# A 64-channel chunk kept as two token halves on 128 partitions, its first layer in array halves, and other due times

## The chip, the cores and the metric

The kernel runs on one core of a Trainium2 chip. The metric is the device time of one execution in microseconds (us), the median of three runs for the kernel before. "PE" is the tensor engine, "ACT" the scalar engine, "DVE" the vector engine, "POOL" the GpSimd engine, and "SP" the engine that only issues transfers here. A PE instruction is either a weight load (LDWEIGHTS) or a matmul (MATMUL).

## The reference

```python
def _A_ref(u, log_A_real, A_imag, C_real, C_imag, log_dt, D_skip):
    dt = jnp.exp(log_dt)
    A = -jnp.exp(log_A_real) + 1j * A_imag
    C = (C_real + 1j * C_imag) * dt[:, None]
    P = jnp.exp((A * dt[:, None])[:, :, None] * pos[None, None, :])
    K = 2.0 * jnp.einsum("dn,dnl->dl", C, P).real
    ...          # y = causal convolution of u with K over 2048 positions
    return y + u * D_skip[None, None, :]

def _B_ref(x, w1, b1, w2):
    h = jnp.einsum("bsd,df->bsf", x, w1) + b1
    sp = jnp.log1p(jnp.exp(-jnp.abs(h))) + jnp.where(h > 0, h, jnp.zeros_like(h))
    act = h * jnp.tanh(sp)
    return jnp.einsum("bsf,fd->bsd", act, w2)

x = A_u                                    # 1 x 2048 x 640
xn = _layernorm(x, axis=-1)
return x + _A_ref(xn, ...) + _B_ref(xn, B_w1, B_b1, B_w2)   # w1 640 x 1728, w2 1728 x 640
```

## The kernel before

The 2048 tokens are handled in four blocks (`b`) of 512; CA and CB are the first and the last 256 tokens of a block. The 640 input channels are five slices (`k`) of 128. The 1728 hidden channels are 14 chunks (`f`): 13 of 128 and, as `f` = 8, one of 64.

To keep float32 accuracy with float16 products, each operand is a high part plus a low part, and a product is three: high by high, low by high, high by low. So a full chunk of the first layer is 15 matmuls of 128x512 into one PSUM bank, and the same for the second layer, which adds into five banks ACC that hold the block's output. In blocks 1 to 3 the chunks 0 to 7 and 9 to 12 are taken two at a time (`PAIRS`); such a pair is computed from seven smaller products of sums of weights and sums of inputs, in parts called `one`, `two`, `three_a`, `three_b` and `four`, of 12, 15, 9, 9 and 9 matmuls of 128x256. Between them ACT copies two results out (`cV`, line 1063, and `cY`, line 1064) before `two` may start, and DVE adds them up (`z`, line 1067, before `three_a`; `w`, line 1071, before `four`). Chunks 8 and 13 of every block, and all of block 0, go one at a time.

Behind each first-layer chunk runs a chain on ACT and DVE: a sigmoid (`sig`), its product with the biased value (`mul`), three more activations (`mish_a1` to `a3`), a product (`mish_v3`), and the split into a high part (`mish_a4`) and a low part (`mish_v4`), which the second layer reads three chunks later.

The chunk of 64 channels has its high and low weights side by side in one 128-wide tile. Its five high-input products are full 128x512 matmuls: the result's partitions 0 to 63 hold the high-weight part, 64 to 127 the low-weight part. The five low-input products have only 64 weight columns, and are laid into the two column halves of the array, two at a time. So one sum stands on 64 partitions by 512 tokens, in two pieces: `half_a` (ACT) copies the upper piece down, `half_v` (DVE) adds the two, and all of the chain works on 64 partitions by 512 tokens. `mish_a4` writes the high part twice, into both partition halves of two tiles, since the second layer wants high and low side by side.

The order of all work after the first 20.8 us is made by a planner (`Plan`) when the program is built. The PE order is written out by hand in `whole`; for ACT, DVE, POOL and SP the planner takes, of what is ready, the operation with the earliest due time. Due times come backwards from the PE order and from numbers written in `whole`: the scan of the state-space part (`skip_a` to `skip_e`, 20 slices of 512 tokens) is spread between `edge` marks, the parameter sums (`mode_ops`) and the checks on the weights (`chk`) have marks of their own. A general path that runs when a check fails stands behind the rest, and isn't taken here.

The PSUM banks H[0], H[1] and TR hold first-layer results. PZ, the place of a pair's last sum, is the CB half of H[0]; chunk 8 uses all of H[1] in block 0 and all of H[0] later.

Of the kernel before, what the change touches and what calls it, by code (L numbers as in the profile page):

```python
# [16 lines left out]
AF = mybir.ActivationFunctionType  # L17
OP = mybir.AluOpType
AX = mybir.AxisListType

P = 128
# [4 lines left out]
TB = 512  # L26
NB = L // TB
NT = TB // P
KD = D // P
FC = [P] * 8 + [64] + [P] * 5  # L30
# [5 lines left out]
PAIRS = (0, 2, 4, 6, 9, 11)  # L36
# [6 lines left out]
MA, MG, MD, MC = -6.52763197, 0.11462477, 0.92081132, 5.9480018 / -6.52763197  # L43
# [16 lines left out]
class Plan:  # L60
# [392 lines left out]
def body(ctx: ExitStack, tc: tile.TileContext, x, xT, logA, Aim, Cr, Ci, logdt, vec, w1, w1T, w2, w2T, out):  # L453
# [58 lines left out]


    TR, *H = (ps.tile([P, TB], F32, name=n) for n in ("tr", "h0", "h1"))
    PV, PX, PZ, PY, PW = TR[:, CA], TR[:, CB], H[0][:, CB], H[1][:, CA], H[1][:, CB]
    PVS = tmp.tile([P, TB // 2], F32, name="pvs")
    ACC = [ps.tile([P, TB], F32, name=f"acc{k}") for k in range(KD)]
    XT, ACT, SM, NX = ({} for _ in range(4))
# [272 lines left out]
    def mm1(b, f):  # L791
        h = bank(b, f)
        n = FC[f]
        xh, xl = XH[b % 2], XL[b % 2]
        hh, lh, hl = ([(h, w[f][:, k], x[k]) for k in range(KD)] for w, x in ((W1H, xh), (W1L, xh), (W1H, xl)))
        if n < P:

            low = [(h[n * (k % 2):n * (k % 2 + 1)], w[:, :n], x) for k, (_, w, x) in enumerate(hl[:-1])]
            _, w, x = hl[-1]
            low += [(h[n * j:n * (j + 1), c], w[:, :n], x[:, c]) for j, c in enumerate((CA, CB))]  # L800
            order = hh[:1] + low + hh[1:]
        elif b == 0:
            order = hh + hl + lh
        else:
            order = [t for pair in zip(hh, lh) for t in pair] + hl
        for j, (o, w, x) in enumerate(order):
            pe.matmul(o, w, x, start=(j == 0), stop=(j == len(order) - 1))  # L807
# [73 lines left out]
        pe.matmul(o, W2H[f][:, c], lo, start=False, stop=f == LAST)  # L881


    def src(b, f):
        return pl["A", b, f][:FC[f]] if FC[f] < P else bank(b, f)

    def half_a(b, f):
        n = FC[f]
        a.copy(pl["A", b, f][:n], bank(b, f)[n:2 * n])

    def half_v(b, f):
        n = FC[f]
        v.tensor_tensor(pl["A", b, f][:n], bank(b, f)[:n], pl["A", b, f][:n], op=OP.add)

    def sig(b, f, h=None, c=slice(0, TB)):
        n = FC[f]
        a.activation(pl["s", b, f][:n, c], src(b, f) if h is None else h, AF.Sigmoid, bias=cv[:n, f:f + 1], scale=1 / SH)  # L897

    def mul(b, f, h=None, c=slice(0, TB)):
        n = FC[f]  # L900
        v.scalar_tensor_tensor(pl["A", b, f][:n, c], src(b, f) if h is None else h, bs[:n, f:f + 1], pl["s", b, f][:n, c],  # L901
                               op0=OP.add, op1=OP.mult)

    def mish_a1(b, f):
        n = FC[f]
        a.activation(pl["p", b, f][:n], pl["s", b, f][:n], AF.Arctan, bias=one[:n], scale=-1.0)  # L906

    def mish_a2(b, f):
        n = FC[f]
        p = pl["p", b, f][:n]  # L910
        a.activation(p, p, AF.Square, bias=pi4[:n], scale=2.0)  # L911

    def mish_a3(b, f):
        n = FC[f]
        p = pl["p", b, f][:n]
        a.activation(p, p, AF.Tanh, bias=mb[:n], scale=MG)  # L916

    def mish_v3(b, f):
        n = FC[f]
        A = pl["A", b, f][:n]  # L920
        v.scalar_tensor_tensor(A, pl["p", b, f][:n], MC, A, op0=OP.add, op1=OP.mult)  # L921

    def mish_a4(b, f):
        n = FC[f]
        A = pl["A", b, f][:n]
        hi = pl["h", b, f][0]
        ACT[f] = hi, None
        a.activation(hi[:n], A, AF.Copy, scale=MA * SA / SH)  # L928
        if n < P:
            hi2 = pl["h", b, f][1]  # L930
            ACT[f] = hi, hi2
            a.activation(hi2[n:2 * n], A, AF.Copy, scale=MA * SA / SH)

    def mish_v4(b, f):
        n = FC[f]
        A = pl["A", b, f][:n]
        hi, hi2 = ACT[f]
        lo = pl["h", b, f][1] if n == P else hi[n:2 * n]
        v.scalar_tensor_tensor(lo, A, MA * SA / SH, hi[:n], op0=OP.mult, op1=OP.subtract)  # L939
        ACT[f] = hi, lo if n == P else hi2  # L940

    def drain(b, k, src, t=slice(0, TB)):
        z = XT[b][:, k, t]
# [3 lines left out]
    def whole():  # L947

        A, V, M, S, G = "ACT", "DVE", "PE", "SP", "POOL"
        M5, M2 = 0.2157, 0.11  # L950
        add = lambda name, eng, cost, fn, *args, **kw: pl.add(name, eng, cost, lambda: fn(*args), **kw)
        nothing = lambda: None
        PAIRED = [f + j for f in PAIRS for j in range(2)]
# [2 lines left out]
        def chain(b, f, pre, drop=()):  # L956

            n = (b, f)
            if FC[f] < P:
                add(("hc", *n), A, 0.55, half_a, b, f, pre=pre, take=("A", ("A", *n), 1))  # L960
                add(("ha", *n), V, 0.62, half_v, b, f, pre=[("hc", *n)])
                add(("sg", *n), A, 0.64, sig, b, f, pre=[("ha", *n)], take=("s", ("s", *n), 2))
                add(("v1", *n), V, 0.68, mul, b, f, pre=[("sg", *n)], drop=[("s", *n)])
            elif b > 0 and f in PAIRS:
                add(("sX", *n), A, 0.36, sig, b, f, PX, CA, pre=[("two", *n)], take=("s", ("s", *n), 2))
                add(("vX", *n), V, 0.38, mul, b, f, PX, CA, pre=[("sX", *n)], take=("A", ("A", *n), 1))
                add(("sg", *n), A, 0.36, sig, b, f, PZ, CB, pre=[("three_b", *n), ("sX", *n)])
                add(("v1", *n), V, 0.38, mul, b, f, PZ, CB, pre=[("sg", *n), ("vX", *n)], drop=[("s", *n)])
            else:
                add(("sg", *n), A, 0.60, sig, b, f, pre=pre, take=("s", ("s", *n), 2))  # L970
                add(("v1", *n), V, 0.68, mul, b, f, pre=[("sg", *n)], take=("A", ("A", *n), 1), drop=[("s", *n)])
            add(("a1", *n), A, 0.63, mish_a1, b, f, pre=[("sg", *n)], take=("p", ("p", *n), 1), drop=[("s", *n)])
            add(("a2", *n), A, 0.63, mish_a2, b, f, pre=[("a1", *n)])
            add(("a3", *n), A, 0.63, mish_a3, b, f, pre=[("a2", *n)])
            add(("v3", *n), V, 0.61, mish_v3, b, f, pre=[("a3", *n), ("v1", *n)], drop=[("p", *n)])
            add(("a4", *n), A, 0.54 if FC[f] == P else 1.1, mish_a4, b, f, pre=[("v3", *n)], take=("h", ("h", *n), 1))
            add(("v4", *n), V, 0.62, mish_v4, b, f, pre=[("a4", *n)], drop=[("A", *n)])

        def second(b, f, parts):

# [35 lines left out]
            chain(0, f, [("m1", 0, f)])  # L1016
        for f in range(3, NF):
            prev = {3: 0, 4: 1}.get(f, f - 2)
            add(("m1", 0, f), M, 15 * M5 if FC[f] == P else 1.85, mm1, 0, f,
                pre=[("hw1", f), ("ow1", f), ("v1", 0, prev), ("sg", 0, prev)] if f > 3 else [("v1", 0, prev), ("sg", 0, prev)])  # L1020
            chain(0, f, [("m1", 0, f)])
            if f == 7:
                add(("spread", 1), M, 0.1, spread, pre=[("rs", 1)])
            for o in second(0, f - LAG, []):
                o()
# [5 lines left out]
        for b in range(1, NB):  # L1031
            for f in range(NF):
# [4 lines left out]
                h2 = (b, f + 1 - LAG) if f + 1 >= LAG else (b - 1, NF + f + 1 - LAG)  # L1037
                if f not in PAIRS:
                    pb = before(b, f)
                    add(("m1", *n), M, 15 * M5 if FC[f] == P else 1.85, mm1, b, f,  # L1040
                        pre=[("v1", b, f - 2), ("sg", b, f - 2)])
# [345 lines left out]
```

## Time and profile before

| what | us |
|---|---|
| three runs | 358.28, 358.29 (median), 358.55 |
| the profiled execution, its own time | 358.88 |
| its span, first to last instruction | 357.3 |
| PE busy in the span | 351.0 |
| DVE, ACT, POOL busy | 311.3, 296.4, 50.5 |
| mean granted clock of PE | 1.000 |

The profiled execution took 358.88 - 357.3 = 1.58 us outside its span, and was 0.59 us longer than the median. The views used are the page, the waits, the chain that ended last in order of time, the groups by shape, and stretches of the timeline. A row of the timeline is start, length, engine, line, operation, tiles and shape, then the count of instructions merged into it; lengths overlap, since an engine begins the next instruction before the last has fully ended, so the distance between two starts tells the pace.

### The profile page before, as it was taken

What the parts mean: (1) busy time and instruction counts of PE and PEld (TensorE: products, weight loads), DVE (VectorE), ACT (ScalarE), POOL (GpSimd) and SP (SyncE); (2) the same over time, 40 slices, a digit from 0 to 9 for tenths busy, and PEclk for the clock granted to TensorE, in tenths of its full rate; (3) what the DMA queues carried; (4) which work ended last, traced back from release to release, by engine and by line L of the source; (5) the groups of instructions that cost most, each with busy time, mean ns of one, the idle gap of its engine ahead of it and who ended that gap; (6) DMA issues with size and microseconds to landing.
All of it is one profiled execution on the core that took longest, in us unless ns stands there. A gap on an engine that the chain in (4) does not pass through costs nothing.

```text
span 357.3 us, 6015 instructions
## 1 busy us (share of the span) xinstructions
PE 351.0 (98%) x2167; PEld 211.6 (59%) x2167; DVE 311.3 (87%) x585; ACT 296.4 (83%) x614; POOL 50.5 (14%) x72
## 2 busy tenths in 40 slices
PE   7999999999999999999999999999999999999996
PEld 6754444444666665666566666466566666567543
DVE  4989989999998999999999997899997988775552
ACT  3599999978487799889989987989988989878750
POOL 2100020000004041100103343100002462000000
PEclk9999999999999999999999999999999999999999
DMA  7889975205109954902255973951110995302004
GB/s 222 293 240 281 348 225 163 113 1 172 50 3 199 318 177 120 292 35 57 60 183 112 187 208 93 246 204 35 33 35 4 160 194 125 81 0 33 0 4 151
DMA packets 26052, 48.75 MB, mean 136 GB/s; under 512 B 3592, under 2 KB 6944, under 8 KB 26016
## 3 DMA queue, kind: packets, MB, share of 16 engines
q1 hardware_dynamic: 19168, 34.21, 29.9%
q0 software_dynamic: 6240, 13.11, 17.9%
q10 hardware_dynamic: 608, 0.98, 0.9%
q8 instruction: 19, 0.31, 0.4%
q14 instruction: 17, 0.14, 0.2%
HBM read 39.10 MB, written 5.26 MB: 124 GB/s over the span
## 4 chain that ended last, share of the span: by engine, by line
PE 95%; DMA 2%; DVE 1%; ACT 1%; issue 0%; ACTq 0%
PE acc L859 48%; PE h L827 18%; PE h L807 14%; PE tr L827 12%; DMA w<-in_w_dram 2%; PE h L789 1%; PE tr L789 1%; PE acc L1251 0%; DVE st L627 0%; PE acc L873 0%; PE acc L870 0%; PE acc L871 0%; ACTq L1271 0%; DVE st L628 0%; ACT w1h L552 0%
## 5 line engine op out<-in xcount | busy, mean ns | idle before, releaser
L859 PE MATMUL acc<-hi,w2h 128*128 128x512 f16 x273 | 100.9, 379 | 0.0
L859 PE MATMUL acc<-hi,w2l 128*128 128x512 f16 (+1 forms) x265 | 99.7, 379 | 0.0
L859 PE MATMUL acc<-lo,w2h 128*128 128x512 f16 x253 | 93.3, 379 | 0.0
L859 PEld LDWEIGHTS <-w2h 128*128 128x128 f16 x526 | 51.2, 98 | 48.5 <-issue 1.3
L897 ACT ACTIVATE s<-h,cv 128x512 f32<-128x512 f32 (+1 forms) x51 | 30.9, 605 | 23.7 <-PE h L827 18.4
L827 PEld LDWEIGHTS <-w1h 128*128 128x128 f16 x432 | 42.3, 98 | 10.7
L921 DVE SCALAR_TENSOR_TENSOR A<-p,A 128x512 f32<-128x512 f32 (+1 forms) x56 | 38.4, 685 | 7.2 <-ACT p L916 7.0
L859 PEld LDWEIGHTS <-w2l 128*128 128x128 f16 x273 | 25.6, 98 | 30.8 <-issue 1.1
L906 ACT ACTIVATE p<-s,kc 128x512 f32<-128x512 f32 (+1 forms) x56 | 40.1, 716 | 0.5
L916 ACT ACTIVATE p<-p,kc 128x512 f32<-128x512 f32 (+1 forms) x56 | 40.1, 715 | 0.2
L911 ACT ACTIVATE p<-p,kc 128x512 f32<-128x512 f32 (+1 forms) x56 | 40.0, 714 | 0.2
L939 DVE SCALAR_TENSOR_TENSOR lo<-A,hi 128x512 f16<-128x512 f32 x52 | 35.5, 682 | 3.6 <-ACT hi L928 3.3
L901 DVE SCALAR_TENSOR_TENSOR A<-h,bs,s 128x512 f32<-128x512 f32 (+1 forms) x51 | 33.1, 649 | 6.2 <-ACT s L897 5.9
L928 ACT ACTIVATE hi<-A 128x512 f16<-128x512 f32 (+1 forms) x56 | 35.0, 624 | 3.6 <-DVE A L921 3.4
L548 POOL DMA_DIRECT2D r<-in_xT_dram x15 | 13.7, 1099 | 126.0 <-ACT r L770 60.3
L807 PEld LDWEIGHTS <-w1h 128*128 128x128 f16 (+1 forms) x174 | 15.3, 99 | 20.3 <-issue 3.3
L749 DVE TENSOR_TENSOR_SCAN g<-g,car,kc 128x512 f32<-128x512 f32 x20 | 25.6, 1280 | 1.1 <-ACT g L743 1.1
L827 PEld LDWEIGHTS <-w1l 128*128 128x128 f16 x216 | 21.1, 98 | 8.4 <-issue 0.3
L753 DVE TENSOR_TENSOR_SCAN g<-g,car,g 128x512 f32<-128x512 f32 x20 | 25.6, 1279 | 0.1
L827 PE MATMUL tr<-xh,w1h 128*128 128x256 f16 x90 | 24.5, 272 | 0.1
L827 PE MATMUL tr<-xh,w1l 128*128 128x256 f16 x90 | 24.5, 273 | 0.0
L827 PE MATMUL tr<-xl,w1h 128*128 128x256 f16 x90 | 24.5, 273 | 0.0
(174 smaller groups left out, 730.1 us busy)
## 6 DMA issues: line engine op xcount, KB each, us to landing
w<-in_w_dram SPq DMA_DIRECT2D x23, 320.0 KB, 4.4
w<-in_w2T_dram SPq DMA_DIRECT2D x15, 288.0 KB, 6.5
w<-in_B_w_dram SPq DMA_DIRECT2D x13, 320.0 KB, 4.0
w<-in_w1T_dram SPq DMA_DIRECT2D x13, 320.0 KB, 6.7
x<-in_A_u_dram SPq DMA_DIRECT2D x12, 320.0 KB, 4.9
xt<-in_xT_dram SPq DMA_DIRECT2D x15, 256.0 KB, 5.6
r<-in_xT_dram POOLq DMA_DIRECT2D x15, 256.0 KB, 6.2
xt<-r POOLq DMA_DIRECT2D x15, 256.0 KB, 3.9
```

What stands on the lines that cost most here:

```text
L749: v.tensor_tensor_scan(g1[:, 1:], g1[:, 1:], zero.to_broadcast([P, TB]), car[:, 1, k:k + 1], op0=OP.add, op1=OP.add)
L807: pe.matmul(o, w, x, start=(j == 0), stop=(j == len(order) - 1))
L827: pe.matmul(o, p, q, start=start and n == 1, stop=n == 3 * len(w), skip_group_check=True)
L859: pe.matmul(o, w, x, start=start, stop=stop)
L897: a.activation(pl["s", b, f][:n, c], src(b, f) if h is None else h, AF.Sigmoid, bias=cv[:n, f:f + 1], scale=1 / SH)
L901: v.scalar_tensor_tensor(pl["A", b, f][:n, c], src(b, f) if h is None else h, bs[:n, f:f + 1], pl["s", b, f][:n, c], op0=OP.add, op1=OP.mult)
L906: a.activation(pl["p", b, f][:n], pl["s", b, f][:n], AF.Arctan, bias=one[:n], scale=-1.0)
L911: a.activation(p, p, AF.Square, bias=pi4[:n], scale=2.0)
L916: a.activation(p, p, AF.Tanh, bias=mb[:n], scale=MG)
L921: v.scalar_tensor_tensor(A, pl["p", b, f][:n], MC, A, op0=OP.add, op1=OP.mult)
L928: a.activation(hi[:n], A, AF.Copy, scale=MA * SA / SH)
L939: v.scalar_tensor_tensor(lo, A, MA * SA / SH, hi[:n], op0=OP.mult, op1=OP.subtract)
```

## The change

The chunk of 64 channels is laid out otherwise. Its 15 products (high by high, low by high, high by low, for five slices) all have 64 weight columns now, and each is done twice: tokens CA into partitions 0 to 63 through one column half of the array, tokens CB into partitions 64 to 127 through the other, both into the CA columns of the bank. So there are 30 matmuls of 64x256 instead of 5 of 128x512, 4 of 64x512 and 2 of 64x256. The sum stands on 128 partitions by 256 columns at once: `half_a` and `half_v` go, the chain works on 128x256, and only `mish_a4` and `mish_v4` go back to 64 partitions, in four and two instructions of 64x256 instead of two and one of 64x512. PZ moves to the CA half of H[0]. In the planner the costs of this chunk's operations are new, `mode_ops` are due before the last chunk of block 0 instead of before chunk 4 of block 1, four of the five scan marks move, and the checks' window goes from chunk 4 of block 1 to chunk 11 of block 3 over to chunk 6 of block 1 to chunk 8 of block 3. Lines of the changed kernel stand up to 14 lower.

```diff
-    PV, PX, PZ, PY, PW = TR[:, CA], TR[:, CB], H[0][:, CB], H[1][:, CA], H[1][:, CB]
+    PV, PX, PZ, PY, PW = TR[:, CA], TR[:, CB], H[0][:, CA], H[1][:, CA], H[1][:, CB]
...
         if n < P:
-            low = [(h[n * (k % 2):n * (k % 2 + 1)], w[:, :n], x) for k, (_, w, x) in enumerate(hl[:-1])]
-            _, w, x = hl[-1]
-            low += [(h[n * j:n * (j + 1), c], w[:, :n], x[:, c]) for j, c in enumerate((CA, CB))]
-            order = hh[:1] + low + hh[1:]
-        elif b == 0:
+            for i, (_, w, x) in enumerate(hh + lh + hl):
+                for j, c in enumerate((CA, CB)):
+                    pe.matmul(h[n * j:n * (j + 1), CA], w[:, :n], x[:, c], start=i == 0, stop=i == 3 * KD - 1)
+            return
+        if b == 0:
...
-    def half_a(b, f):
-        n = FC[f]
-        a.copy(pl["A", b, f][:n], bank(b, f)[n:2 * n])
-
-    def half_v(b, f):
-        n = FC[f]
-        v.tensor_tensor(pl["A", b, f][:n], bank(b, f)[:n], pl["A", b, f][:n], op=OP.add)
...
+    def cols(f):
+        return slice(0, TB) if FC[f] == P else CA
...
     def mish_a4(b, f):
...
+        for t in (hi[:n], lo[n:2 * n]):
+            for j, c in enumerate((CA, CB)):
+                a.activation(t[:, c], A[n * j:n * (j + 1), CA], AF.Copy, scale=MA * SA / SH)
     def mish_v4(b, f):
...
+        for j, (c, h) in enumerate(((CA, hi[:n]), (CB, lo[n:2 * n]))):
+            v.scalar_tensor_tensor(hi[n:2 * n, c], A[n * j:n * (j + 1), CA], MA * SA / SH, h[:, c], op0=OP.mult, op1=OP.subtract)
...
+        HALF1 = 1.84
...
-            if FC[f] < P:
-                add(("hc", *n), A, 0.55, half_a, b, f, pre=pre, take=("A", ("A", *n), 1))
-                add(("ha", *n), V, 0.62, half_v, b, f, pre=[("hc", *n)])
...
-            add(("m1", 0, f), M, 15 * M5 if FC[f] == P else 1.85, mm1, 0, f,
+            add(("m1", 0, f), M, 15 * M5 if FC[f] == P else HALF1, mm1, 0, f,
...
-                due=start(1, 4))
+                due=start(0, 13))
...
-        edge = [start(1, 4), start(2, 0), start(2, 11), start(3, 5), start(3, 11)]
+        edge = [start(0, 13), start(2, 0), start(2, 8), start(3, 8), start(3, 13)]
...
-        t0, t1 = start(1, 4), start(3, 11)
+        t0, t1 = start(1, 6), start(3, 8)
```

What the planner makes of it is shown at three places. The first is PE at the beginning of chunk 8 in block 0 (`w1h8` are the chunk's weights, `xh00` to `xh04` and `xl00` to `xl04` the high and low inputs of the five slices, `h1` the bank). Before:

```order
L807 LDWEIGHTS w1h8_121
L807 MATMUL h1_212<-xh00_168,w1h8_121 128x512
L807 LDWEIGHTS w1h8_121
L807 MATMUL h1_212<-xl00_178,w1h8_121 64x512
L807 LDWEIGHTS w1h8_121
L807 MATMUL h1_212<-xl01_179,w1h8_121 64x512
L807 LDWEIGHTS w1h8_121
L807 MATMUL h1_212<-xl02_180,w1h8_121 64x512
```

and now:

```order
L800 LDWEIGHTS w1h8_121
L800 MATMUL h1_212<-xh00_168,w1h8_121 64x256
L800 LDWEIGHTS w1h8_121
L800 MATMUL h1_212<-xh00_168,w1h8_121 64x256
L800 LDWEIGHTS w1h8_121
L800 MATMUL h1_212<-xh01_169,w1h8_121 64x256
L800 LDWEIGHTS w1h8_121
L800 MATMUL h1_212<-xh01_169,w1h8_121 64x256
```

Each 64-column load now serves a matmul of 256 tokens, and nothing in the chunk is 128 columns wide any more.

The second is ACT in block 1 around the copies of the second pair (chunks 2 and 3): `pvs<-tr` is `cV`, `h1<-tr` is `cY`, `p1` is the chain of an earlier chunk. Before:

```order
L897 ACTIVATE s1_243<-h1_212,cv_102 128x512
L906 ACTIVATE p1_248<-s1_243,kc_89 128x512
L928 ACTIVATE hi2_253<-A2_246 128x512
L911 ACTIVATE p1_248<-p1_248,kc_89 128x512
L1063 COPY pvs_213<-tr_210 128x256
L1064 COPY h1_212<-tr_210 128x256
L916 ACTIVATE p1_248<-p1_248,kc_89 128x512
```

and now:

```order
L890 ACTIVATE s1_243<-h1_212,cv_102 128x512
L898 ACTIVATE p1_248<-s1_243,kc_89 128x512
L598 ACTIVATE swh1_189<-t3_232 128x256
L902 ACTIVATE p1_248<-p1_248,kc_89 128x512
L1049 COPY pvs_213<-tr_210 128x256
L906 ACTIVATE p1_248<-p1_248,kc_89 128x512
L1050 COPY h1_212<-tr_210 128x256
```

One activation of 128x512 has come between the two copies.

The third is DVE for the same pair, ahead of `z` (`h0<-h1,pvs`); `r<-acc0` and `r<-acc1` take the last block's sums out of ACC, `lo2` the low part of a chunk, `swl1` the low part of this pair's weight sums. Before:

```order
L629 BN_AGGR mv_1268<-st_1270 128x2
L768 TENSOR_SCALAR r1_236<-acc0_214 128x512
L768 TENSOR_SCALAR r2_237<-acc1_215 128x512
L1067 TENSOR_TENSOR h0_211<-h1_212,pvs_213 128x256
L683 TENSOR_REDUCE ok_455<-mx_453 128x1
```

and now:

```order
L768 TENSOR_SCALAR r0_235<-acc0_214 128x512
L926 SCALAR_TENSOR_TENSOR lo2_254<-A2_246,hi2_253 128x512
L768 TENSOR_SCALAR r2_237<-acc1_215 128x512
L602 SCALAR_TENSOR_TENSOR swl1_195<-t2_231,swh1_189 128x512
L1053 TENSOR_TENSOR h0_211<-h1_212,pvs_213 128x256
```

Two more instructions of 128x512 stand between the taking out of ACC and `z`.

More of the change, by code (lines that the diff above doesn't have):

```diff
@@ L881, in mm2_half @@
         pe.matmul(o, W2H[f][:, c], lo, start=False, stop=f == LAST)
-    def src(b, f):
-        return pl["A", b, f][:FC[f]] if FC[f] < P else bank(b, f)
-    def half_a(b, f):
-        n = FC[f]
-        a.copy(pl["A", b, f][:n], bank(b, f)[n:2 * n])
-    def half_v(b, f):
-        n = FC[f]
[L893 to L897, printed above, removed]
@@ L899, in mul, with sig @@
-    def mul(b, f, h=None, c=slice(0, TB)):
-        n = FC[f]
-        v.scalar_tensor_tensor(pl["A", b, f][:n, c], src(b, f) if h is None else h, bs[:n, f:f + 1], pl["s", b, f][:n, c],
+    def cols(f):
+        return slice(0, TB) if FC[f] == P else CA
+    def sig(b, f, h=None, c=None):
+        c = c or cols(f)
+        a.activation(pl["s", b, f][:, c], bank(b, f)[:, c] if h is None else h, AF.Sigmoid, bias=cv[:, f:f + 1], scale=1 / SH)
+    def mul(b, f, h=None, c=None):
+        c = c or cols(f)
+        v.scalar_tensor_tensor(pl["A", b, f][:, c], bank(b, f)[:, c] if h is None else h, bs[:, f:f + 1], pl["s", b, f][:, c],
@@ L902, in mul @@
                                op0=OP.add, op1=OP.mult)
     def mish_a1(b, f):
-        n = FC[f]
-        a.activation(pl["p", b, f][:n], pl["s", b, f][:n], AF.Arctan, bias=one[:n], scale=-1.0)
+        a.activation(pl["p", b, f][:, cols(f)], pl["s", b, f][:, cols(f)], AF.Arctan, bias=one, scale=-1.0)
     def mish_a2(b, f):
-        n = FC[f]
-        p = pl["p", b, f][:n]
-        a.activation(p, p, AF.Square, bias=pi4[:n], scale=2.0)
+        p = pl["p", b, f][:, cols(f)]
+        a.activation(p, p, AF.Square, bias=pi4, scale=2.0)
@@ L913, in mish_a3 @@
     def mish_a3(b, f):
-        n = FC[f]
-        p = pl["p", b, f][:n]
-        a.activation(p, p, AF.Tanh, bias=mb[:n], scale=MG)
+        p = pl["p", b, f][:, cols(f)]
+        a.activation(p, p, AF.Tanh, bias=mb, scale=MG)
     def mish_v3(b, f):
-        n = FC[f]
-        A = pl["A", b, f][:n]
-        v.scalar_tensor_tensor(A, pl["p", b, f][:n], MC, A, op0=OP.add, op1=OP.mult)
+        A = pl["A", b, f][:, cols(f)]
+        v.scalar_tensor_tensor(A, pl["p", b, f][:, cols(f)], MC, A, op0=OP.add, op1=OP.mult)
@@ L923, in mish_a4 @@
     def mish_a4(b, f):
[L924 to L932, printed above, removed]
-    def mish_v4(b, f):
[L935 to L940, printed above, removed]
+        hi, lo = ACT[f] = pl["h", b, f]
@@ new lines, in mish_a4 @@
+        A, n = pl["A", b, f], FC[f]
+        if n == P:
+            a.activation(hi, A, AF.Copy, scale=MA * SA / SH)
+            return
+        for t in (hi[:n], lo[n:2 * n]):
+            for j, c in enumerate((CA, CB)):
+                a.activation(t[:, c], A[n * j:n * (j + 1), CA], AF.Copy, scale=MA * SA / SH)
+    def mish_v4(b, f):
+        hi, lo = ACT[f]
+        A, n = pl["A", b, f], FC[f]
+        if n == P:
+            v.scalar_tensor_tensor(lo, A, MA * SA / SH, hi, op0=OP.mult, op1=OP.subtract)
+            return
+        for j, (c, h) in enumerate(((CA, hi[:n]), (CB, lo[n:2 * n]))):
+            v.scalar_tensor_tensor(hi[n:2 * n, c], A[n * j:n * (j + 1), CA], MA * SA / SH, h[:, c], op0=OP.mult, op1=OP.subtract)
@@ L958, in chain @@
             n = (b, f)
-            if FC[f] < P:
-                add(("hc", *n), A, 0.55, half_a, b, f, pre=pre, take=("A", ("A", *n), 1))
-                add(("ha", *n), V, 0.62, half_v, b, f, pre=[("hc", *n)])
-                add(("sg", *n), A, 0.64, sig, b, f, pre=[("ha", *n)], take=("s", ("s", *n), 2))
-                add(("v1", *n), V, 0.68, mul, b, f, pre=[("sg", *n)], drop=[("s", *n)])
-            elif b > 0 and f in PAIRS:
+            t = (lambda one, half: one if FC[f] == P else half)
+            if b > 0 and f in PAIRS:
                 add(("sX", *n), A, 0.36, sig, b, f, PX, CA, pre=[("two", *n)], take=("s", ("s", *n), 2))
@@ L969, in chain @@
             else:
[L970 to L977, printed above, removed]
+                add(("sg", *n), A, t(0.60, 0.36), sig, b, f, pre=pre, take=("s", ("s", *n), 2))
+                add(("v1", *n), V, t(0.68, 0.38), mul, b, f, pre=[("sg", *n)], take=("A", ("A", *n), 1), drop=[("s", *n)])
+            add(("a1", *n), A, t(0.63, 0.36), mish_a1, b, f, pre=[("sg", *n)], take=("p", ("p", *n), 1), drop=[("s", *n)])
+            add(("a2", *n), A, t(0.63, 0.36), mish_a2, b, f, pre=[("a1", *n)])
+            add(("a3", *n), A, t(0.63, 0.36), mish_a3, b, f, pre=[("a2", *n)])
+            add(("v3", *n), V, t(0.61, 0.36), mish_v3, b, f, pre=[("a3", *n), ("v1", *n)], drop=[("p", *n)])
+            add(("a4", *n), A, t(0.54, 1.44), mish_a4, b, f, pre=[("v3", *n)], take=("h", ("h", *n), 1))
+            add(("v4", *n), V, t(0.62, 0.80), mish_v4, b, f, pre=[("a4", *n)], drop=[("A", *n)])
         def second(b, f, parts):
@@ L1039, in whole @@
                     pb = before(b, f)
-                    add(("m1", *n), M, 15 * M5 if FC[f] == P else 1.85, mm1, b, f,
+                    add(("m1", *n), M, 15 * M5 if FC[f] == P else HALF1, mm1, b, f,
                         pre=[("v1", b, f - 2), ("sg", b, f - 2)])
```

## The prediction

> **What bounds the kernel now.** I read the page first, then the waits of PE, then the busy time by stage, and last the chain that ended last. The page:
>
> ```profile
> span 357.3 us, 6015 instructions
> PE 351.0 (98%) x2167; PEld 211.6 (59%) x2167; DVE 311.3 (87%) x585; ACT 296.4 (83%) x614; POOL 50.5 (14%) x72
> ...
> PE 95%; DMA 2%; DVE 1%; ACT 1%; issue 0%; ACTq 0%
> ```
>
> PE is busy for 351.0 of 357.3 us and 95% of the last chain is PE. All waits of PE that the trace has (engine and line that waited, whom for, us in total, times, longest):
>
> ```profile
> PE tr L1265 <- POOL car L494: 1.7, 1, 1.7
> PE acc L1251 <- DVE x L1235: 0.4, 2, 0.3
> PE h L789 <- DVE w1l L556: 0.3, 1, 0.3
> PE tr L789 <- ACT w1h L552: 0.2, 1, 0.2
> ```
>
> The four lines belong to the first 20 us, which the change leaves as they are. By stage (length of the stretch, then busy us and instructions of each engine):
>
> ```profile
> 21.00:53.78 32.78, 32.78 (x155) 14.84 (x152) 30.36 (x64) 32.72 (x53) 2.17 (x3) 1.00 0.89 283
> 53.78:90.00 36.22, 36.22 (x173) 16.00 (x172) 35.08 (x62) 32.46 (x65) 0.00 (x0) 1.00 0.34 112
> 90.00:174.90 84.90, 84.84 (x559) 53.72 (x558) 81.91 (x176) 72.27 (x154) 13.53 (x17) 1.00 0.48 134
> 174.90:259.50 84.60, 84.60 (x559) 53.62 (x557) 77.99 (x128) 76.66 (x171) 14.98 (x19) 1.00 0.53 141
> 259.50:344.00 84.50, 84.50 (x559) 53.55 (x557) 64.17 (x108) 70.62 (x153) 16.12 (x20) 1.00 0.34 67
> ```
>
> The columns behind the length are PE, weight loads, DVE, ACT and POOL, then granted clock and DMA. From 21 to 344 us PE is busy all the time but for 0.06 us. So two things set the time: how long the PE stream itself is, and whether a hand-over from ACT or DVE comes so late that PE has its first wait. ACT (32.72 of 32.78 us) and DVE (35.08 of 36.22, then 81.91 of 84.90) are nearly full in blocks 0 and 1, so the second question is open there.
>
> **The PE stream.** The chain that ended last, in order of time, gives a whole chunk at once (start, us, line, matmuls):
>
> ```profile
> 50.70 3.24 PE acc L859 x15
> 53.94 1.85 PE h L807 x11
> ...
> 100.19 0.98 PE h L827 x9
> ...
> 139.69 1.85 PE h L807 x11
> ...
> 224.50 1.85 PE h L807 x11
> ...
> 308.99 1.85 PE h L807 x11
> ```
>
> A matmul of 512 tokens costs 3.24 / 15 = 0.216 us, one of 256 tokens 0.98 / 9 = 0.109, and the chunk of 64 channels 1.85 in each of the four blocks. What is inside these 1.85 us is seen in the timeline of block 0 (merged rows, so a row's start counts):
>
> ```profile
> 53.78 0.38 PE L807 MATMUL h<-xh,w1h 128*128 128x512 f16 x1
> 54.09 0.41 PE L807 MATMUL h<-xl,w1h 128*64 128x512 f16 x2
> 54.33 0.38 PE L807 MATMUL h<-xl,w1h 128*64 128x512 f16 x2
> 54.54 0.28 PE L807 MATMUL h<-xl,w1h 128*64 128x256 f16 x2
> 54.75 0.39 PE L807 MATMUL h<-xh,w1h 128*128 128x512 f16 x1
> ...
> 54.09 0.14 PEld L807 LDWEIGHTS <-w1h 128*64 128x64 f16 x4 [0.42 <-issue]
> ...
> 54.33 0.11 PEld L807 LDWEIGHTS <-w1h 128*64 128x64 f16 x2
> ```
>
> From full width to halves, 53.78 to 54.09 is 0.31, so 0.09 more than a 512-token matmul. The first pair of halves takes 0.24, 0.02 more than 0.216: its loads have no cover. The second pair takes 0.21, as long as one matmul: the halves do run side by side. The pair of 256 tokens takes 54.54 to 54.75 = 0.21, which is 0.109 and 0.10 for the way back to full width.
>
> The new chunk has the same one way in and one way back, the same uncovered first load, and 15 pairs of 256 tokens where before stood five full matmuls and two pairs of 512 tokens and a pair of 256. The difference is 15 x 0.109 - 7 x 0.216 - 0.109 = 1.635 - 1.512 - 0.109 = +0.014 us per block, and 4 x 0.014 = **+0.06 us** in all. This holds if 15 pairs in a row keep the 0.109. The trace has just one such pair, between others. The lower bound: no 256-token matmul in the rows is faster than 0.109, so no gain. The near bound above: the two loads of the next pair start with the pair before and are recorded as 0.11 long, up to 0.115 behind the first matmul's start; if the next pair waits for the recorded end, it costs 15 x 0.006 = 0.09 per block, +0.36 more. The far bound: load and matmul in turn, 0.11 + 0.109 = 0.22 per pair, 15 x 0.11 = 1.65 per block, +6.6. The same figure comes out if instructions are supplied no faster than where the trace keeps it up for long, one load and one matmul per 0.109 (the nine of 100.19 us): a pair needs two of each. I take the lowest, since after the uncovered first load, recorded as 0.11 too, the matmuls were only 0.02 late: the recorded length is not what a matmul waits for.
>
> **ACT and DVE.** The groups by shape (count, busy us, mean ns):
>
> ```profile
> L893 DVE TENSOR_TENSOR A<-h,A 64x512 f32<-64x512 f32 x4 | 2.7, 680 | 1.1 <-ACT A L889 1.1
> L897 ACT ACTIVATE s<-A,cv 64x512 f32<-64x512 f32 x4 | 2.9, 719 | 0.1
> L906 ACT ACTIVATE p<-s,kc 64x512 f32<-64x512 f32 x4 | 2.8, 711 | 0.0
> L932 ACT ACTIVATE lo<-A 64x512 f16<-64x512 f32 x4 | 2.5, 628 | 0.1
> L598 ACT ACTIVATE swh<-t 128x256 f16<-128x256 f32 x6 | 2.4, 407 | 0.0
> L602 DVE SCALAR_TENSOR_TENSOR swl<-t,swh 128x256 f16<-128x256 f32 x6 | 2.5, 421 | 0.0
> ```
>
> Per block, ACT loses a copy (about 0.6 like the others), its sigmoid and three activations go from 0.71 to about 0.41 (4 x 0.30 = 1.2), and the splitting goes from 2 x 0.63 to 4 x 0.41, 0.4 more: about 1.4 us less. DVE loses the 0.68 of the sum, two products go from about 0.68 to 0.42, and the low part from 0.68 to 2 x 0.42: about 1.0 less. Over four blocks that is some 5 and 4 us. Both lie under PE's work, and PE waits for neither, so they are worth **0**; only if the new order made PE wait could they give some of that back. PZ's move keeps its operations and the waits' order; 0.
>
> The new order does move hand-overs. Two that I followed, in block 1's second pair. The copies on ACT, and PE's `two`, which needs `cY`:
>
> ```profile
> 103.59 0.71 ACT L911 ACTIVATE p<-p,kc 128x512 f32<-128x512 f32 x1
> 104.21 0.35 ACT L1063 COPY pvs<-tr 128x256 f32<-128x256 f32 x1
> 104.46 0.37 ACT L1064 COPY h<-tr 128x256 f32<-128x256 f32 x1
> ...
> 105.56 0.27 PE L827 MATMUL tr<-xh,w1h 128*128 128x256 f16 x1
> ```
>
> `cY` ends at 104.83, 0.73 us before PE needs it. One activation now stands between the copies; from start to start one takes 104.21 - 103.59 = 0.62. So 0.11 is left. Then `z` on DVE, and `three_a`, which needs it:
>
> ```profile
> 106.27 1.24 DVE L768 TENSOR_SCALAR r<-acc 128x512 f32<-128x512 f32 x2
> 107.47 0.43 DVE L1067 TENSOR_TENSOR h<-h,pvs 128x256 f32<-128x256 f32 x1
> ...
> 109.14 0.27 PE L827 MATMUL h<-th,swh 128*128 128x256 f16 x1
> ```
>
> `z` ends at 107.90, 1.24 before it is needed; two DVE instructions more, at (107.47 - 106.27) / 2 = 0.60 each, leave 0.04. Behind a late `z` in DVE's queue stand the next chain's products, which the second layer reads chunks later, so a late `z` passes on its own lateness only. Both margins stay on the right side, hardly. In the whole order six of the 18 pairs have an activation between the copies now, against three before. The other margins lie between these and about 1 us. Below nothing isn't possible here, since PE had no wait to lose; above, one more instruction of 0.6 in front at each of the two places gives 1.2. I take 0.1, near the rows, which still fit.
>
> The later marks of `edge` put the last scan slices further back in block 3, where DVE has room (64.17 of 84.50). The checks begin later and no transfer is added. After 344 us PE runs to its end and the last stores follow as before: 0.
>
> **The sum.** The profiled execution took 358.88, its span 357.3 and 1.58 around it. 358.88 + 0.06 + 0.1 = 359.04 in its terms. It was 0.59 longer than the median of 358.29, so the median should become 358.45, say **358.5**.
>
> **The rivals.** *Pairs don't keep the 0.109* (slower). Thirty loads and thirty matmuls want an instruction every 27 ns for 1.6 us; the rows show such a rate for six instructions only (four loads and two matmuls from 54.09 us on). Load and matmul in turn gives 358.5 + 6.6 = 365.1; it decides from 0.12 per pair on. For it: no row shows even two pairs of 256 tokens in a row. Against it: the loads at 54.33 run under the matmuls of 54.33, in both halves. The Trainium skill, "TensorE: Matmul & The Clock Gate", in Part 3 on what overlaps, says that a load overlaps matmuls under way only when its row group differs; here all loads use all rows, so by that rule this rival would hold. The trace disagrees with it at 54.33 us.
>
> *Hand-overs come late* (slower). ACT and DVE are full in block 0 and most of block 1, and the planner puts work nearer to its due time. If at the six pairs the copies come one activation late, with 0.11 left, PE waits up to 0.5 at each; at half of that, 6 x 0.25 = 1.5, the time is about 359.9. It decides from 0.6 us of waits in all. Against it: about 1.4 and 1.0 us of work less per block.
>
> *The halves cost no change of shape* (faster). If a chunk all in halves had neither the 0.09 nor the 0.10, PE would save 4 x 0.19 = 0.76: 357.7. Nothing speaks for it; both neighbours of the chunk stay full width.
>
> *The freed ACT and DVE time reaches the end* (faster): bounded by PE's waits after 21 us, 0.06. The time stays 358.4.
>
> **How the numbers follow.** The forecast, with the near bound on the pairs (358.9) and the last rival inside it, has 0.57; pairs that are slower 0.12; late hand-overs 0.24; the faster one 0.05; 0.02 remain for either side. A measurement of this kernel tells apart about 0.2%, 0.7 us, so same is 357.6 to 359.0. Faster 0.06, same 0.57, slower 0.37. The forecast's own range is 358.1 to 359.0. The range for 8 in 10 leaves out most of the faster case and the far end of the slow pairs, and takes in late hand-overs up to 2 us: 357.9 to 360.6.
>
> **What would show it.** Right: chunk 8 takes 1.86 in each block, its pairs start 0.109 apart, PE has no wait after 21 us, and ACT and DVE are busy some 5 and 4 us less. Wrong: pairs 0.12 or more apart; a chunk of 2 us or more; waits of PE for `cY` or `z`, above all in block 1; or an end after the last matmul that is longer than before.

## The result: no change that counts, +0.14% in one series and +0.03% in the next

The changed kernel took 358.93 us (median of 22 runs, 358.40 to 360.20), the kernel before 358.44 beside it (22 runs, 357.99 to 359.06): a ratio of 1.0014, 95% interval 1.0008 to 1.0021. In a second series of both it was 358.61 us (11 runs) against 358.47 (24 runs), ratio 1.0003, interval 0.9994 to 1.0012. The prediction was 358.5.

The profiled execution of the change had 358.76 us and a span of 356.8, so 1.96 us lie outside its span, where the kernel before had 1.58. The page of the change:

```profile
span 356.8 us, 6183 instructions
PE 350.1 (98%) x2243; PEld 214.4 (60%) x2243; DVE 307.5 (86%) x585; ACT 293.6 (82%) x618; POOL 49.2 (14%) x72
...
PE 96%; DVE 2%; DMA 1%; ACT 0%; POOL 0%; issue 0%
```

PE is about as busy as before (350.1 us, before 351.0), DVE 3.8 us and ACT 2.8 us less. Its waits (engine and line that waited, whom for, us in total, times, longest):

```profile
PE tr L1251 <- POOL ident masks.py:199: 1.7, 1, 1.7
PE acc L1237 <- DVE x L1221: 1.2, 3, 0.8
PE h L789 <- ACT w1h L552: 0.2, 1, 0.2
```

All three belong to the first 20 us, as before. The chain that ended last, in order of time (start, us, line, matmuls), has chunk 8 in the four blocks as:

```profile
53.53 1.76 PE h L800 x30
...
139.30 1.76 PE h L800 x30
...
223.90 1.76 PE h L800 x30
...
308.40 1.76 PE h L800 x30
```

and the timeline of PE in block 0 shows what is in it (merged rows; a row's start counts):

```profile
53.15 0.38 PE L859 MATMUL acc<-hi,w2l 128*128 128x512 f16 x1
53.46 1.28 PE L800 MATMUL h<-xh,w1h 128*64 128x256 f16 x20
54.58 0.71 PE L800 MATMUL h<-xl,w1h 128*64 128x256 f16 x10
55.22 0.39 PE L859 MATMUL acc<-hi,w2h 128*128 128x512 f16 x1
```

From the last full matmul to the first halves it is 0.31, 0.09 over the pace; ten pairs then take 54.58 - 53.46 = 1.12, so 0.109 each and 0.02 for the first load; the five others and the way back to full width take 0.64. Together 0.09 + 1.76 = 1.85 us, as much as before within the 0.02 that these rows can tell.

How long is the PE stream as a whole? Two rows of the timeline give it in each kernel: the first full matmul of the planned part, and the last matmul. Before:

```profile
21.30 0.59 PE L807 MATMUL h<-xh,w1h 128*128 128x512 f16 x2
...
353.59 0.27 PE L881 MATMUL h<-lo,w2h 128*128 128x256 f16 x1
```

and the change:

```profile
20.88 1.03 PE L807 MATMUL h<-xh,w1h 128*128 128x512 f16 x4
...
353.02 0.27 PE L881 MATMUL h<-lo,w2h 128*128 128x256 f16 x1
```

353.59 - 21.30 = 332.29 us before, 353.02 - 20.88 = 332.14 now: 0.15 shorter. The start itself, 21.30 or 20.88, isn't a property of either kernel: in three profiles of the kernel before (one of them with idle SP instructions, as told below) it was 20.73 to 21.30, in the six of the change's PE order without waits 20.76 to 21.26. What scatters in the work ahead of it was not followed. The streams don't scatter: 332.29 us in each of those three profiles, and 332.14 in each of those six.

The 0.15 has two parts. The distance between starts shows one wait in the kernel before that the list of waits doesn't have, late in block 1:

```profile
159.37 0.38 PE L859 MATMUL acc<-hi,w2l 128*128 128x512 f16 x1
159.81 0.27 PE L827 MATMUL tr<-xh,w1h 128*128 128x256 f16 x1
...
158.49 0.37 ACT L1063 COPY pvs<-tr 128x256 f32<-128x256 f32 x1 [0.53 <-PE tr L827]
158.76 0.73 ACT L916 ACTIVATE p<-p,kc 128x512 f32<-128x512 f32 x1
159.39 0.38 ACT L1064 COPY h<-tr 128x256 f32<-128x256 f32 x1
```

From 159.37 to 159.81 is 0.44 where a matmul of 512 tokens takes 0.216: PE waited 0.22 us for `cY`, which ended at 159.39 + 0.38 = 159.77, behind an activation between the copies. A PE row's length is modelled and runs on past the next start, so the wait was filled in the busy time. In the change the same place reads:

```profile
158.99 0.38 PE L859 MATMUL acc<-hi,w2l 128*128 128x512 f16 x1
159.21 0.27 PE L827 MATMUL tr<-xh,w1h 128*128 128x256 f16 x1
...
158.11 0.37 ACT L1049 COPY pvs<-tr 128x256 f32<-128x256 f32 x1 [0.52 <-PE tr L827]
158.38 0.38 ACT L1050 COPY h<-tr 128x256 f32<-128x256 f32 x1
158.69 0.63 ACT L916 ACTIVATE hi<-A 128x512 f16<-128x512 f32 x1
```

The copies follow each other, `cY` is there at 158.76, and PE goes on after 0.22. Read this way, by distances of starts above the usual pace, the change has no wait after 21 us at all. Without its wait the old stream is 332.07, so the new products cost 332.14 - 332.07 = 0.07 us, and the wait saved was 0.22.

So the change's stream is 0.15 us faster, and what it is slower by must be looked for outside the span: 1.95 us there (median of the first 22 runs, 1.88 to 2.05) against 1.55 (24 runs of the kernel before in the second series, 1.50 to 1.69). That makes +0.40, and with the -0.15 a difference of +0.25, between the +0.49 of the first series and the +0.14 of the second. The rest is scatter of the spans: the change's had a median of 357.0 us in the first series and of 356.7 in the second.

### The profile page after: what moved, and what is told of

Its sections match the earlier page's. It is cut to its first block, busy times and chain, and to the rows that moved or that the text cites. A ratio compares the mean times of both kernels' runs of the same rounds, so it can differ in the third digit from the quotient of the medians.

```text
span 356.8 us, 6183 instructions
## 1 busy us (share of the span) xinstructions
PE 350.1 (98%) x2243; PEld 214.4 (60%) x2243; DVE 307.5 (86%) x585; ACT 293.6 (82%) x618; POOL 49.2 (14%) x72
## 4 chain that ended last, share of the span: by engine, by line
PE 96%; DVE 2%; DMA 1%; ACT 0%; POOL 0%; issue 0%
PE acc L859 48%; PE h L827 18%; PE h L807 12%; PE tr L827 12%; PE h L800 2%; PE h L789 1%; DMA x<-in_A_u_dram 1%; PE tr L789 1%; PE acc L1237 0%; ACT xh L1240 0%; DVE st L627 0%; DVE st L628 0%; DVE x L1221 0%; POOL rs L1281 0%; PE acc L871 0%; PE acc L870 0%
## 5 line engine op out<-in xcount | busy, mean ns | idle before, releaser
L890 ACT ACTIVATE s<-h,cv 128x512 f32<-128x512 f32 (+1 forms) x55 | 32.7, 594 | 28.4 <-PE h L827 21.7
L910 DVE SCALAR_TENSOR_TENSOR A<-p,A 128x512 f32<-128x512 f32 (+1 forms) x56 | 37.3, 667 | 8.5 <-ACT p L906 7.9
L902 ACT ACTIVATE p<-p,kc 128x512 f32<-128x512 f32 (+1 forms) x56 | 39.2, 700 | 0.6
L898 ACT ACTIVATE p<-s,kc 128x512 f32<-128x512 f32 (+1 forms) x56 | 39.2, 700 | 0.5
L894 DVE SCALAR_TENSOR_TENSOR A<-h,bs,s 128x512 f32<-128x512 f32 (+1 forms) x55 | 35.0, 639 | 5.3 <-ACT s L890 5.2
L906 ACT ACTIVATE p<-p,kc 128x512 f32<-128x512 f32 (+1 forms) x56 | 39.2, 699 | 0.4
L916 ACT ACTIVATE hi<-A 128x512 f16<-128x512 f32 x52 | 32.3, 622 | 2.1 <-DVE A L910 1.9
L827 PEld LDWEIGHTS <-swh 128*128 128x128 f16 x216 | 21.1, 98 | 4.3
```

The source lines that it names most:

```text
L827: pe.matmul(o, p, q, start=start and n == 1, stop=n == 3 * len(w), skip_group_check=True)
L890: a.activation(pl["s", b, f][:, c], bank(b, f)[:, c] if h is None else h, AF.Sigmoid, bias=cv[:, f:f + 1], scale=1 / SH)
L894: v.scalar_tensor_tensor(pl["A", b, f][:, c], bank(b, f)[:, c] if h is None else h, bs[:, f:f + 1], pl["s", b, f][:, c], op0=OP.add, op1=O ...
L898: a.activation(pl["p", b, f][:, cols(f)], pl["s", b, f][:, cols(f)], AF.Arctan, bias=one, scale=-1.0)
L902: a.activation(p, p, AF.Square, bias=pi4, scale=2.0)
L906: a.activation(p, p, AF.Tanh, bias=mb, scale=MG)
```

## The experiments

Waits below are distances between PE starts above the usual pace after 21 us, without the changes of shape; "outside" is an execution's time less its span, as a median. The instruction counts are of the built program, general path included. No kernel leaves work out; some do a step twice or carry idle instructions, as told.

**Halves and due times apart.** Both kernels again, the halves with the old due times, and the old chunk with the new ones. `e1_layout` against the change; the same three lines the other way, on the kernel before, make `e2_marks`:

```diff
-                due=start(0, 13))
+                due=start(1, 4))
...
-        edge = [start(0, 13), start(2, 0), start(2, 8), start(3, 8), start(3, 13)]
+        edge = [start(1, 4), start(2, 0), start(2, 11), start(3, 5), start(3, 11)]
...
-        t0, t1 = start(1, 6), start(3, 8)
+        t0, t1 = start(1, 4), start(3, 11)
```

> The kernel before, unchanged, in a series of its own. The profiled execution of it took 358.88 us with a span of 357.3, so 1.6 lie outside the span; all 22 runs of the change have 1.9 to 2.0 there. Theory C (the 0.49 us of the change lie outside the span, with the larger program): the runs here have 1.5 to 1.6 outside the span, at the same spans as the change's, 356.5 to 357.2. Theory A (the products cost it, inside the span): the runs have the same 1.6 to 2.0 outside and spans 0.1 to 0.4 shorter than the change's. Theory B (late hand-overs in some runs): its spans scatter less, by 0.3, and the change's by 1 us. Median in any case 358.4.

> The change, unchanged, once more. Ratio 1.001 to 1.002 again. Theory A and C: its profile shows no TensorE wait after 21 us, and the first layer of chunk 8 again takes 1.76 us from its first half product to the next chunk. Theory B: the profile of another execution shows a TensorE wait of 0.1 to 0.6 us after 21 us, for a tile cY or z.

> The change with the three old due times: the halves alone. Theory A: the products bring the whole difference, ratio 1.001 to 1.002 as for the change. Theory B: the new due times bring it, so ratio 1.000 (358.4 us) and no waits. Theory C: 1.001 to 1.002, with 1.9 to 2.0 us outside the span.

> The kernel before with the three new due times and nothing else. Theory A and C: ratio 1.000, 1.5 to 1.6 us outside the span, no TensorE wait after 21 us. Theory B: the due times bring the difference, ratio 1.001 to 1.002, with a wait for cY or z in the profile.

| kernel | chunk 8 | due times | us, median (runs) | ratio to before, interval | waits | outside |
|---|---|---|---|---|---|---|
| `r1_before` | old | old | 358.42 (11) | 1.0001, 0.9992 to 1.0009 | 0.22 | 1.58 |
| `r2_after` | halves | new | 358.61 (11) | 1.0003, 0.9994 to 1.0012 | 0 | 1.96 |
| `e1_layout` | halves | old | 359.67 (6) | 1.0030, 1.0018 to 1.0042 | 1.63 | 1.70 |
| `e2_marks` | old | new | 359.66 (5) | 1.0033, 1.0020 to 1.0045 | 1.33 | 1.75 |

A sixth execution of `e2_marks` took 1313 us and is left out.

The second series of the change, `r2_after`, came out at 1.0003, below the 1.001 to 1.002 that was expected of it; its profile has no wait and 1.96 us outside the span, as theory C has it. That a larger program makes the difference outside is not borne out: `e1_layout` has the change's products and 1.70.

Each half of the change alone costs over a microsecond, and the two together under half of one, none of it in waits. None of the theories had that. The stream without waits is 332.13 us in `e1_layout` and 332.07 in `e2_marks`, the same as its layout has elsewhere, so all of the loss is waits. Two of the three in `e1_layout` are for `cY`; the PE and ACT rows of one:

```profile
147.46 0.38 PE L859 MATMUL acc<-hi,w2l 128*128 128x512 f16 x1
148.18 0.27 PE L827 MATMUL tr<-xh,w1h 128*128 128x256 f16 x1 [0.34 <-ACT h L1050]
...
147.14 0.72 ACT L745 ACTIVATE g<-xt,cc 128x512 f32<-128x512 f32 x1
147.77 0.36 ACT L1050 COPY h<-tr 128x256 f32<-128x256 f32 x1
```

The distance of the PE starts is 0.72, half a microsecond over pace, since a piece of the scan (line 745) was put ahead of the copy. In `e2_marks` the largest wait, 0.82 us, is for a chain's low part, behind statistics on DVE:

```profile
188.59 0.38 PE L859 MATMUL acc<-hi,w2h 128*128 128x512 f16 x1
189.63 0.38 PE L859 MATMUL acc<-lo,w2h 128*128 128x512 f16 x1 [0.66 <-DVE lo L939]
...
188.30 0.47 DVE L628 BATCH_NORM_STATS2 st<-x 128x6 f32<-128x320 f32 x1
188.81 0.21 DVE L629 BATCH_NORM_AGGREGATE mv<-st 128x2 f32<-128x12 f32 x1
188.94 0.64 DVE L939 SCALAR_TENSOR_TENSOR lo<-A,hi 128x512 f16<-128x512 f32 x1
```

**Which of the due times.** From the change, `u1_checks` takes back only the third line of the diff above (the checks' window), `u2_edges` only the first two (parameters and scan).

> The change with the old window of due times for the checks of the weights alone. If the checks' window was what made the halves lose 1.2 us with the old due times: 359.7 and TensorE waits of 1 to 1.6 us after 21 us; if the skip branch's edges were: 358.7 and none. Outside the span 1.9 to 2.0 if SyncE's instruction count decides it (as many as in the change: 258 in the program).

> The change with the old due times of the mode parameters and of the skip branch, and the new window of the checks. If the edges were what made the halves lose 1.2 us: 359.7 and TensorE waits of 1 to 1.6 us after 21 us; if the checks' window was: 358.7 and none. Outside the span 1.75 if SyncE's instruction count decides it (257, as in the kernel before with the new due times, which had 1.75).

`u1_checks`: 358.25 us (10 runs), ratio 0.9996 (0.9986 to 1.0005), no wait, 1.57 outside. `u2_edges`: 360.01 us (5 runs), ratio 1.0036 (1.0022 to 1.0050), 1.52 us of waits, 1.61 outside. The scan's and the parameters' marks, which were not taken apart, are what the halves needed; the checks' window could have stayed. The guess on what lies outside fell in both: `u1_checks` has as many SP instructions as the change and not its 1.95.

**Giving the saved time back.** Chunk 8's four copies and two subtractions are issued twice:

```diff
-        for t in (hi[:n], lo[n:2 * n]):
+        for t in 2 * (hi[:n], lo[n:2 * n]):
...
-        for j, (c, h) in enumerate(((CA, hi[:n]), (CB, lo[n:2 * n]))):
+        for j, (c, h) in 2 * list(enumerate(((CA, hi[:n]), (CB, lo[n:2 * n])))):
...
-            add(("a4", *n), A, t(0.54, 1.44), mish_a4, b, f, pre=[("v3", *n)], take=("h", ("h", *n), 1))
-            add(("v4", *n), V, t(0.62, 0.80), mish_v4, b, f, pre=[("a4", *n)], drop=[("A", *n)])
+            add(("a4", *n), A, t(0.54, 2.88), mish_a4, b, f, pre=[("v3", *n)], take=("h", ("h", *n), 1))
+            add(("v4", *n), V, t(0.62, 1.60), mish_v4, b, f, pre=[("a4", *n)], drop=[("A", *n)])
```

> The change with chunk 8's four copies on ScalarE and its two subtractions on VectorE issued twice (the second time writing the same values), their planned costs doubled: about 1.4 us of ScalarE and 0.7 to 0.8 us of VectorE a block, what the change had saved there and a little less. If the saved time is worth nothing, 358.6 to 358.9 and no TensorE wait over 0.3 after 21 us. If it is worth something, up to 5.6 us more, or a wait of some tenths at the tight hand-overs as in the two mixed kernels (359.7).

Measured: 361.18 us (4 runs), ratio 1.0076 (1.0059 to 1.0092), 1.99 us of waits, and 4.41 us after the last matmul's start where all the others have 3.6 to 3.8. The PE starts go from the pace of 0.22 to 1.31 at the place where the kernel before had lost its 0.22:

```profile
159.06 0.38 PE L859 MATMUL acc<-hi,w2l 128*128 128x512 f16 x1
160.37 0.27 PE L827 MATMUL tr<-xh,w1h 128*128 128x256 f16 x1 [0.93 <-ACT h L1050]
...
158.45 0.72 ACT L745 ACTIVATE g<-xt,cc 128x512 f32<-128x512 f32 x1
159.07 0.35 ACT L1049 COPY pvs<-tr 128x256 f32<-128x256 f32 x1
159.33 0.72 ACT L906 ACTIVATE p<-p,kc 128x512 f32<-128x512 f32 x1
159.95 0.37 ACT L1050 COPY h<-tr 128x256 f32<-128x256 f32 x1
```

With these due times the order does not bear the added work. The run doesn't separate the added work from the order that the planner made of the added cost: both are in it.

**The halves one after the other.** The two loops of the chunk's products are exchanged:

```diff
-            for i, (_, w, x) in enumerate(hh + lh + hl):
-                for j, c in enumerate((CA, CB)):
+            for j, c in enumerate((CA, CB)):
+                for i, (_, w, x) in enumerate(hh + lh + hl):
```

> The change with the 15 products of chunk 8's upper half first and those of the lower half after them, instead of in pairs; nothing else. Theory A (the array halves work side by side only when the two halves' products alternate, and a half product takes 0.109 by itself too): 15 x 0.109 more a block, 6.5 in all, so 365.2 us, with the 30 products of a chunk over 3.27 + 0.19 instead of 1.86 us. Rival (the load of a half's next weights cannot lie under the products of the same half): 0.109 + 0.106 for each, 30 x 0.215 = 6.45 a chunk, 18 us more, 377. Rival (order does not matter): 358.7.

Measured: 363.50 us (4 runs), ratio 1.0139 (1.0122 to 1.0156), no waits. The chain has each chunk at 2.99 instead of 1.76:

```profile
53.45 2.99 PE h L800 x30
...
140.44 2.99 PE h L800 x30
```

4 x 1.23 = 4.9 us more, and the stream is 337.05 instead of 332.14, 4.91. So the order matters, and PE's time goes through to the end one for one. But strictly one after the other the chunk would be 30 x 0.109 + 0.12 = 3.39, with the same first load and way back, and 2.99 is 0.40 less, nearly four pitches. The timeline of PE shows why, where the upper half's last products (`xl`) meet the lower half's first (`xh`):

```profile
54.49 0.38 PE L800 MATMUL h<-xl,w1h 128*64 128x256 f16 x2
54.61 0.30 PE L800 MATMUL h<-xh,w1h 128*64 128x256 f16 x1
54.71 0.27 PE L800 MATMUL h<-xl,w1h 128*64 128x256 f16 x1
54.74 0.27 PE L800 MATMUL h<-xh,w1h 128*64 128x256 f16 x1
54.82 0.27 PE L800 MATMUL h<-xl,w1h 128*64 128x256 f16 x1
54.85 0.27 PE L800 MATMUL h<-xh,w1h 128*64 128x256 f16 x1
54.93 0.27 PE L800 MATMUL h<-xl,w1h 128*64 128x256 f16 x1
```

In the program all 15 products of the upper half come first. Here products of the lower half start at 54.61, 54.74 and 54.85, ahead of `xl` products that stand before them: the idle half was served early. And the loads of one half lie under its own products:

```profile
53.38 1.28 PE L800 MATMUL h<-xh,w1h 128*64 128x256 f16 x10
...
53.38 1.01 PEld L800 LDWEIGHTS <-w1h 128*64 128x64 f16 x10 [0.42 <-issue]
```

The ten `xh` products of the upper half start between 53.38 and the first `xl` at 54.49, at 1.11 / 10 = 0.11 each, and the ten loads that the window has run in the same time, in the same half and on the same 128 rows. Load and product in turn would have taken 0.22 each. The rival of 377 us falls. Theory A, 365.2, was right that order matters and 1.7 us too long, since it had no overlap where the halves meet.

**What lies outside the span.** Eight kernels so far, with values between 1.55 and 2.04 us, each within 0.25 us from run to run. The kernel before with two idle instructions more on SP, and the change with one:

> The kernel before with two drain instructions more on SyncE at its end, all other engines as before: 257 SyncE instructions in the program, where the kernel before has 255, the change with the old due times 256, the kernel before with the new ones 257, and the change 258. Their times outside the span are 1.55, 1.70, 1.75 and 1.95 us. If SyncE's count decides that part: 1.75 here. If another engine's count or the products do: 1.55.

> The change with one drain instruction more on SyncE at its end, all other engines as in the change: 259 SyncE instructions. If SyncE's count decides the time outside the span: over 2.0, or back to 1.55 if it goes in steps of four. If not: 1.95.

1.57 and 1.95 us (9 runs each): nothing moved, so SP's count is not it. `u1_checks` then differs from the change in its counts only by five instructions on ACT (1484 against 1489) and three on DVE (686 against 689), beside the order. `q1_act5` and `q2_dve3` add these as idle drains at the end of the one engine or the other:

```diff
     pl.run()
+    for _ in range(3):
+        v.drain(fusable=False)
     rv = NX.get("rv")
```

> The change with the old window of the checks, which had 1.57 us outside the span and no waits, with five drain instructions more on ScalarE at its end: now every engine has as many instructions in the program as in the change but VectorE (686, the change 689). If ScalarE's count makes the change's 1.95 us outside the span: 1.95 here, 358.65 us in all. If VectorE's count, or the order of the work, does: 1.57 and 358.3. If both engines add their part: between, about 1.75.

> The same kernel with three drain instructions more on VectorE at its end instead: all counts as in the change but ScalarE's (1484, the change 1489). If VectorE's count makes the 1.95 us outside the span: 1.95 here, 358.65 us in all. If ScalarE's, or the order of the work: 1.57 and 358.3. If both add: about 1.75. In either kernel no TensorE wait after 21 us, since the planned order is that of a kernel that had none.

| kernel | DVE instructions | outside | us, median (runs) |
|---|---|---|---|
| `u1_checks` | 686 | 1.57 | 358.25 (10) |
| `q1_act5` (5 more on ACT) | 686 | 1.57 | 358.14 (10) |
| `q2_dve3` (3 more on DVE) | 689 | 1.95 | 358.67 (10) |
| the change | 689 | 1.95 | 358.93 (22) |

Three idle instructions on DVE bring the change's 0.38 us, to the hundredth, and five on ACT bring nothing. By what rule isn't settled: with 684, 687, 696, 697 and 701 instructions on DVE the values are 1.55, 1.75, 1.70, 1.61 and 1.69, which is not a line, and `e3_in_turn` has 2.04 with 689.

`q1_act5` has the lowest median of all kernels here, 358.14 us, ratio 0.9993 (0.9983 to 1.0003): under the change, and not told apart from the kernel before.

## Why the prediction was right

- **The PE stream, +0.06.** Measured +0.07. Fifteen pairs in a row keep the 0.109, as the lowest of the three bounds had it: the first ten take 1.12. The near bound (0.115) and the far one (0.22) are both refuted. The Trainium skill's rule ("TensorE: Matmul & The Clock Gate", Part 3), by which loads overlap matmuls only with another row group, doesn't hold here: `e3_in_turn` has ten loads on the same rows under ten products. Even with the halves in turn the far bound's 6.6 is only 4.9.
- **ACT's and DVE's saved time, worth 0.** Right for the sum, and half of the story. The saving was 3.8 us on DVE as said (some 4), and 2.8 on ACT instead of some 5: the activations of 128x256 take 0.50 and not the 0.41 that was taken from a scaling, 12 x 0.09 = 1.1 us of it; the rest of the gap was not looked into.

```profile
L898 ACT ACTIVATE p<-s,kc 128x256 f32<-128x256 f32 x4 | 2.0, 502 | 0.0
```

  It doesn't shorten PE. Whether the new due times hold only with it was not shown, though two runs fit that: the new due times without the saved time cost 1.33 us of waits (`e2_marks`), and with it given back 1.99 (`e4_twice`). In both the planner's order changed along with the work, so an order that any change of costs upsets explains them as well.
- **The hand-overs, +0.1.** The sign failed. "Below nothing isn't possible here, since PE had no wait to lose" rested on PE's busy time, which hid the 0.22 us at 159.6. The new order lost that wait and made no other. What made it go, the freed time or the order, isn't separated: neither `e1_layout` nor `e2_marks` has it. The margins that were said to shrink to 0.11 and 0.04 were 0.45 and 0.92: `cY` of block 1's second pair ends at 104.35 + 0.37 = 104.72 for a PE start at 105.17, `z` at 107.40 + 0.43 = 107.83 for 108.75.

```profile
104.35 0.37 ACT L1050 COPY h<-tr 128x256 f32<-128x256 f32 x1
...
105.17 0.27 PE L827 MATMUL tr<-xh,w1h 128*128 128x256 f16 x1
...
107.40 0.43 DVE L1053 TENSOR_TENSOR h<-h,pvs 128x256 f32<-128x256 f32 x1
...
108.75 0.27 PE L827 MATMUL h<-th,swh 128*128 128x256 f16 x1
```

  The reckoning put the added instructions in front of each hand-over and left out that the queue ahead of it had become shorter. It also followed two hand-overs of one pair and took the others to be no tighter: over all 18 pairs `cY` ended 0.05 to 1.10 us before PE's start in the kernel before, the 0.05 being the wait at 159.81, and 0.44 to 1.10 in the change.
- **Around the span, 0.** This failed, by +0.40: the prediction carried the 1.58 us over as if they belonged to the chip. They change with the program: three idle instructions on DVE alone moved them by 0.38.
- **The sum, 358.5.** +0.07 - 0.22 + 0.40 = +0.25, between the two series. The 0.4 us that the first series lies above the forecast are mostly the part outside the span. That the sum came so near is in part luck: the forecast had neither the 0.22 nor the 0.40, and they partly cancel.
- **The rivals.** Late hand-overs did not happen in the change, but happen in four of its neighbours, at 359.7 to 361.2 us, near the 359.9 that was worked out. The sum agrees better than the mechanism: the price was six waits of 0.25 us for the copies, and these kernels have three to five waits of up to 1.09 us, some of them for a chain's parts (`e2_marks` has none for `cY`). Of the two faster rivals, halves without a change of shape did not show: both ways were paid in full, 0.09 and 0.10. The other was bounded by PE's waits at 0.06 us, and this bound was too low, as 0.22 us was there to lose.

## What to carry to other kernels

Due times of a planner may fit only the costs that they were set for: here the new layout with the old times, and the new times with the old layout, each lost over 1 us that the two together don't lose, so measure both parts apart before one is kept or dropped. Read waits of PE from the distance between starts, since its busy time can cover them. Where a change is worth tenths of a microsecond, take the time outside the span from each run first, as idle instructions alone moved it by 0.38 us.

## What the runs showed of the hardware

- PE takes matmuls for an idle column half of the array out of order: in `e3_in_turn` products of the lower half started at 54.61, 54.74 and 54.85, among those of the upper half that stand before them in the program, and the chunk was 0.40 us shorter than strictly in turn. The Trainium skill ("TensorE: Matmul & The Clock Gate", Part 3) says that matmuls keep the program's order in start and end; the starts here disagree.
- The time outside the span is a kernel's own, between 1.55 and 2.04 us here. Three idle instructions on DVE moved it from 1.57 to 1.95 us, five on ACT and one or two on SP did not move it; by what rule is open, as `e3_in_turn` has 2.04 with the change's count of 689 on DVE.
- Going from full width to halves or back costs PE 0.09 to 0.10 us, whichever kernel it is in: in all profiles of this study 16 such changes, of columns in chunk 8's first layer and of rows in its second, add up to 1.51 us from 21 us on, in both layouts.
